# Layer 2's g@w_out of the last two tile pairs by seven block products

## The chip, the cores and the metric

The kernel runs on one core of a Trainium2 chip, in one launch. The metric is device time in microseconds; the median of several executions is compared. The trace and the profile are of one execution of the same program.

## What is computed

An attention over chunks of 32 rows, and two feed-forward layers behind it, all in fp32:

```python
q, k, v: (4, 8, 768, 64)      # chunk 32, 16 rows of left and 8 of right context, 8 memory rows
for c in range(768 // 32):
    scores = q_c @ concat(mem_k, k_ctx).T / 8
    out[:, :, c] = softmax(scores) @ concat(mem_v, v_ctx)
x = out.transpose(0, 2, 1, 3).reshape(3072, 512)
for layer in (1, 2):                              # w_in 512 x 2048, w_out 2048 x 512
    h = x @ w_in
    g = h * clip(h + 3, 0, 6) / 6                 # layer 1
    g = where(h >= 1, h, where(h <= -1, 0, (h + 1)**2 / 4))   # layer 2
    x = g @ w_out
```

## The kernel before

**Tiles.** The 3072 tokens are six tiles of 512 (T). d_ff is 16 blocks f of 128 (NF), d_model four chunks of 128 (NC). Each fp32 operand is split into two fp32r parts (a high part by a ScalarE cast, a low part by a VectorE subtraction), and a product is three matmuls: high by high, high by low, low by high. The function `split` does this for g; it writes ghi and glo, of which there are three buffers each.

**Stages.** Attention of the first tile and the packed weights come first, then layer 1 of tiles 0 and 1 in the direct way (`hidden`, `project`) with attention of the others in between. The rest is five tile pairs, numbered by layer (0 or 1) and pair: (0,1), (0,2), (1,0), (1,1), (1,2). The text says "layer 2" for l = 1.

**A pair.** For eight i (each two blocks f) `hidden_pair` makes h = x @ w_in of both tiles by seven products of half-size blocks instead of eight (Strassen's scheme in Winograd's form): operands A11, A12, S1 to S4, A22 made by `pair_x` on VectorE and ScalarE out of the two tiles of x, weights B11, B21, B22, T1 to T4 made beforehand by `combine` and `weight_pair`. Each product is six matmuls (2 chunks x 3) into a PSUM bank X, W or Z, with ScalarE copies and VectorE additions between products. `gate` applies the activation: ScalarE (relu, and in layer 2 a square) and VectorE. The pair's first tile goes through `project` as g comes out; the second tile's g is kept in SBUF (g_parts) and goes through `project` after the last i, 16 blocks f after one another, while the next pair's operands are made.

**w_out in layer 2.** `project` lets g stand and w_out move: y[128 tokens, 512] += ghi[:, 128 tokens].T @ w_out, for four token chunks, three matmuls each. y has four PSUM banks ("y"); the hidden products have four others ("h", "a"). After the last f each y is copied to SBUF and stored, 256 KB at a time.

**Weights.** They come packed in 64-bit words and are unpacked (`decoded`) on ScalarE and VectorE; layer 2's w_out is unpacked by `weight(1, f, 1, ...)` beside pair (1,0), used there, and written back to DRAM (`wos`) for later loads of 512 KB by `load_out`.

**Order.** A planner (`Plan`) writes out the order of every engine's instructions ahead: each task has a key (its due place), a cost in ns and buffers out of pools: "w" has 32 slots of 4 KB a partition, "in" and "lv" two larger ones each. A share such as ("wo", 5) limits how many slots one kind of buffer may hold. Engines then run these orders strictly, and all loads and stores go through one queue, SP's.

Of the kernel before, what the change touches and what calls it, by code (L numbers as in the profile page):

```python
# [36 lines left out]
T = 512  # L37
# [194 lines left out]
def dve(n, fast=False):  # L232
    return 70 + n / (1.92 if fast else 0.96)


def act(n, psum=False):
    return (30 if psum else 60) + n * 0.9
# [3 lines left out]
def fused_kernel(ctx: ExitStack, tc: tile.TileContext, qkv, qk, vv, wpk, const, out):  # L241
# [23 lines left out]
    wfs = dram.tile([NF // 2, 4, 128, 1024], F32, name="wfs")  # L265
    wos = dram.tile([2, NF, 128, 2, 512], F32, name="wos")

    plan = Plan({**shapes, **banks})
# [24 lines left out]
    def decoded(l, f, z, key, after, raw):  # L293
# [27 lines left out]
        return lo, hi  # L321

    def weight(l, f, z, key, after=()):
# [7 lines left out]
        lo, hi = decoded(l, f, z, key, after, raw)  # L331

        def high(e):
            cast(e, tile_of(w)[:, 0], words(raw)[2][:, 1])

        def low(e):
            t = tile_of(w)
            V.tensor_tensor(out=t[:, 1], in0=words(raw)[2][:, 1], in1=t[:, 0], op=ALU.subtract)

        add(("ACT", 560), key - 0.2, high, [hi], [(w, 0)])  # L340
        t = add(("DVE", dve(512)), key - 0.1, low, [hi, (w, 0)], [(w, 1)])
        if l == 0:
            last_w.append(t)
        if l:
            keep(l, f, z, key + 1)

    def keep(l, f, z, key, after=()):
# [70 lines left out]
    def weight_pair(i, key, after):  # L418
# [31 lines left out]
        for x, b in enumerate(bs):  # L450
            m = 256 * b.shape[1]
            add(
                ("SP", 430), key + 0.2, lambda e, x=x, b=b, m=m: nc.sync.dma_start(
                    wfs[i, x, :, :m], flat(tile_of(b)).bitcast(F32)),
                [(b, y) for y in range(1 + x // 2)], [("wfs", i, x)], kb=m / 2,
            )

# [340 lines left out]
    def project(l, n, f, key, w, ghi, glo, first, last):  # L798
# [154 lines left out]
    def gate(l, p, t, f, key, h, psum=False):  # L953
        r = Buf(["r"], [128, T], F32, "r")
        if t == 0:
            g, view = h, (lambda: tile_of(h))
        else:
            if (l, p, f // 2) not in g_parts:
                g_parts[l, p, f // 2] = Buf(["w"], [128, 2, T], F32, "g")
            g = g_parts[l, p, f // 2]  # L960
            view = lambda: tile_of(g)[:, f % 2]
# [7 lines left out]
        of = (h, 0) if t == 0 else (g, f % 2)  # L969
        add(("DVE", dve(T)), key + 0.1, lambda e: V.scalar_tensor_tensor(  # L970
            out=view(), in0=tile_of(r), scalar=1.0 if l else 6.0, in1=tile_of(h), op0=ALU.min,
            op1=ALU.max if l else ALU.mult,
        ), [(r, 0)] + [(h, 0)] * t, [of])
        raw_g[l, p, t, f] = view, of

    raw_g = {}


# [47 lines left out]
    for n, (l, p) in enumerate(pairs):  # L1026
        base = NK + 30 * n
        for i in range(NF // 2):
            k = base + step * i
            if n:  # L1030
                load_pair(l, p, i, k - 6, [done[n - 1, i]])
            elif i > 1:
                combine(i, k - 2, [done[0, i - 2 if i < KEPT else i - 3]])
            done[n, i] = hidden_pair(l, p, i, k - 1.2 * (n == 4 and i == NF // 2 - 1))
            for x in range(2):
                f = 2 * i + x
# [6 lines left out]
                project(l, 2 * p, f, key, w, *split(key - 1.5, *raw_g[l, p, 0, f]), f == 0, f == NF - 1)  # L1043
        for j in range(NF):
            f = (j + NF - 4) % NF
            key = base + 24.75 + 0.5 * j
            w = w_of[f] if j < 4 else load_out(l, f, key - 5, [done[n, j // 2]])
            project(l, 2 * p + 1, f, key, w, *split(key - 2, *raw_g[l, p, 1, f]), j == 0, j == NF - 1)
        if n + 1 < len(pairs):
            pair_x(*pairs[n + 1], base + 25, [done[n, 5]])  # L1050
        if n == 1:
            for i in range(NF // 2):
                weight_pair(i, base + 4 + 3 * i, [done[1, max(i - 1, 0)]])
                for x in range(2):
                    weight(1, 2 * i + x, 1, base + 30 + step * (i + 0.5 * x) - 3, [done[1, 6]])

# [98 lines left out]
```

## Time and profile before

| | us |
|---|---|
| median of 3 runs (lowest, highest) | 1117.31 (1115.94, 1119.04) |
| the profiled execution, and its span from first to last instruction | 1116.86, 1114.8 |
| TensorE busy, weight loads busy | 1078.8, 880.1 |
| VectorE busy, ScalarE busy | 678.4, 601.7 |

Busy time is the union of an engine's instructions. A matmul's listed duration is longer than the distance to the next one's start, so instructions of TensorE overlap and its busy time hides small gaps. The rows that matter stand below.

### The profile page before, as it was taken

What the parts mean: (1) busy time and instruction counts of PE and PEld (TensorE: products, weight loads), DVE (VectorE), ACT (ScalarE), POOL (GpSimd) and SP (SyncE); (2) the same over time, 40 slices, a digit from 0 to 9 for tenths busy, and PEclk for the clock granted to TensorE, in tenths of its full rate; (3) what the DMA queues carried; (4) which work ended last, traced back from release to release, by engine and by line L of the source; (5) the groups of instructions that cost most, each with busy time, mean ns of one, the idle gap of its engine ahead of it and who ended that gap; (6) DMA issues with size and microseconds to landing.
All of it is one profiled execution on the core that took longest, in us unless ns stands there. A gap on an engine that the chain in (4) does not pass through costs nothing.

```text
span 1114.8 us, 21047 instructions
## 1 busy us (share of the span) xinstructions
PE 1078.8 (97%) x8323; PEld 880.1 (79%) x8323; DVE 678.4 (61%) x1185; ACT 601.7 (54%) x1312; POOL 0.2 (0%) x4
## 2 busy tenths in 40 slices
PE   4699999999999999999999999999999999999998
PEld 4578888777787788888878888888888888888887
DVE  2589648866997976487797465572344562443442
ACT  3499534554665554376675477672455652555531
POOL 0000000000000000000000000000000000000000
PEclk9999999999999999999999999999999999999999
DMA  6792159887977739499999497754576264764061
GB/s 195 263 399 68 42 192 342 295 288 257 314 253 253 249 85 374 146 388 412 414 384 414 173 335 244 267 180 170 215 270 215 104 227 177 274 229 139 1 245 38
DMA packets 108808, 265.63 MB, mean 238 GB/s; under 512 B 11046, under 2 KB 44710, under 8 KB 108710
## 3 DMA queue, kind: packets, MB, share of 16 engines
q1 hardware_dynamic: 108710, 264.29, 65.9%
q8 instruction: 66, 1.08, 0.4%
q14 instruction: 32, 0.26, 0.1%
HBM read 199.23 MB, written 65.01 MB: 237 GB/s over the span
## 4 chain that ended last, share of the span: by engine, by line
PE 75%; DMA 9%; DVE 9%; ACT 3%; issue 2%; SPq 1%; DVEq 0%; ACTq 0%
PE ph L926 9%; PE ph L927 9%; PE ph L928 9%; PE po L815 8%; PE po L813 8%; PE po L814 8%; PE py L808 5%; PE py L809 5%; PE py L810 5%; PE pv L688 2%; PE ph L772 2%; PE ph L773 2%; PE ph L774 2%; DVE tr L667 2%; PE sc L619 1%
## 5 line engine op out<-in xcount | busy, mean ns | idle before, releaser
L926 PE MATMUL ph<-xop,wf 128*128 128x512 f32 x448 | 174.9, 390 | 0.8 <-ACT s L910 0.4
L927 PE MATMUL ph<-xop,wf 128*128 128x512 f32 x448 | 174.3, 389 | 0.0
L928 PE MATMUL ph<-xop,wf 128*128 128x512 f32 x448 | 174.3, 389 | 0.0
L962 ACT ACTIVATE r<-s,bias 128x512 f32<-128x512 f32 x120 | 86.7, 724 | 130.1 <-DVE s L914 129.2
L808 PE MATMUL py<-ghi,w 128*128 128x512 f32 x384 | 152.0, 396 | 0.5 <-DVE ysb L835 0.5
L809 PE MATMUL py<-glo,w 128*128 128x512 f32 x384 | 150.0, 391 | 1.1 <-DVE glo L793 1.1
L815 PE MATMUL po<-w,glo 128*128 128x512 f32 x384 | 149.6, 389 | 0.0
L810 PE MATMUL py<-ghi,w 128*128 128x512 f32 x384 | 149.6, 389 | 0.0
L813 PE MATMUL po<-w,ghi 128*128 128x512 f32 x384 | 149.5, 389 | 0.0
L814 PE MATMUL po<-w,ghi 128*128 128x512 f32 x384 | 149.4, 389 | 0.0
L914 DVE TENSOR_TENSOR s<-s,ph 128x512 f32<-128x512 f32 x120 | 82.0, 685 | 72.2 <-PE ph L928 47.2
L793 DVE TENSOR_TENSOR glo<-g,ghi 128x512 fp32r<-128x512 f32 x80 | 54.7, 690 | 97.5 <-ACT ghi L792 97.4
L792 ACT CAST ghi<-g 128x512 fp32r<-128x512 f32 x80 | 49.2, 622 | 110.6 <-PE po L814 78.6
L926 PEld LDWEIGHTS ph<-xop,wf 128*128 128x128 f32 x448 | 84.1, 188 | 19.7 <-ACT s L910 1.3
L928 PEld LDWEIGHTS ph<-xop,wf 128*128 128x128 f32 x448 | 84.1, 188 | 17.6
L927 PEld LDWEIGHTS ph<-xop,wf 128*128 128x128 f32 x448 | 84.1, 188 | 17.3
L910 ACT COPY s<-ph 128x512 f32<-128x512 f32 x120 | 69.6, 580 | 48.1 <-PE ph L928 44.2
L970 DVE SCALAR_TENSOR_TENSOR s<-r,s 128x512 f32<-128x512 f32 x80 | 55.2, 690 | 49.6 <-ACT r L966 42.4
L808 PEld LDWEIGHTS py<-ghi,w 128*128 128x128 f32 x384 | 72.0, 188 | 16.9 <-DVE ysb L835 1.0
L793 DVE TENSOR_TENSOR glo<-s,ghi 128x512 fp32r<-128x512 f32 x80 | 55.1, 690 | 49.7 <-ACT ghi L792 49.5
L809 PEld LDWEIGHTS py<-glo,w 128*128 128x128 f32 x384 | 72.1, 188 | 16.3 <-DVE glo L793 2.0
L815 PEld LDWEIGHTS po<-w,glo 128*128 128x128 f32 x384 | 72.1, 188 | 15.6 <-DVE glo L793 0.6
(94 smaller groups left out, 1723.4 us busy)
## 6 DMA issues: line engine op xcount, KB each, us to landing
w<-wos SPq DMA_DIRECT2D x124, 512.0 KB
raw<-wpk SPq DMA_DIRECT2D x64, 512.0 KB
wf<-wfs SPq DMA_DIRECT2D x48, 512.0 KB
wf<-wfs SPq DMA_DIRECT2D x48, 384.0 KB
wos<-w SPq DMA_DIRECT2D x32, 512.0 KB
wis<-w SPq DMA_DIRECT2D x16, 512.0 KB
wts<-wt SPq DMA_DIRECT2D x16, 512.0 KB
wf<-wts SPq DMA_DIRECT2D x16, 512.0 KB
```

The lines of the kernel that those rows point to most:

```text
L793: add(("DVE", dve(T)), key + 0.1, lambda e: V.tensor_tensor(out=tile_of(glo), in0=g(), in1=tile_of(ghi), op=ALU.subtract,), [of, (ghi, 0)] ...
L808: P.matmul(y, w2hi, gh, start=first, stop=False)
L809: P.matmul(y, w2hi, gl, start=False, stop=False)
L810: P.matmul(y, w2lo, gh, start=False, stop=last)
L813: P.matmul(y, gh[:, t], wt[:, 0], start=first, stop=False)
L814: P.matmul(y, gh[:, t], wt[:, 1], start=False, stop=False)
L815: P.matmul(y, gl[:, t], wt[:, 0], start=False, stop=last)
L914: add(("DVE", dve(T)), key + 0.39 * j, lambda e: V.tensor_tensor(out=tile_of(s), in0=tile_of(s), in1=tile_of(b), op=ALU.add,), [(b, 0)], [ ...
L926: P.matmul(q, whi()[:, m], xh, start=first, stop=False, skip_group_check=True)
L927: P.matmul(q, whi()[:, m], xl, start=False, stop=False, skip_group_check=True)
L928: P.matmul(q, wlo()[:, m], xh, start=False, stop=c == 1, skip_group_check=True)
L962: add(("ACT", 750 if l else act(T, psum) + 80), key, lambda e: A.activation(out=tile_of(r), in_=tile_of(h), func=AF.Relu, bias=bias[:, l:l ...
```

## The change

For the pairs (1,1) and (1,2) (`SEVEN`) the product g @ w_out is made by seven block products too. The blocks are: rows, the pair's two tiles; inner dimension, f blocks of even and odd index; columns, the two halves of 256 of w_out's permuted columns. One group d takes four blocks f (4d to 4d + 3, the two i = 2d and 2d + 1), with two products x of the scheme accumulated in one bank. w_out now stands (128 columns) and the split operand of 512 tokens moves, so results have output columns on partitions and tokens along the free dimension.

- `combine_out` makes T1 to T4 of w_out, beside pair (1,0), where w_out is unpacked, splits them and stores them (`wcs`). The unpacked w_out itself is stored with its columns permuted (`by_chunk`), so that `project` in pair (1,0) reads it in runs of 32 columns.
- `gate` keeps g of both tiles in g_parts for these pairs (at most nine buffers).
- `out_pair` runs the seven steps of a group: loads of the weights (`load_step`), S1 to S4 on VectorE (`made`), splits, 12 matmuls a step, and additions of PSUM results into SBUF sums (`c_sum`). After a pair's last group VectorE transposes 32 x 32 blocks and SP stores the result. In each group 14 results are taken out of PSUM.
- The last group of (1,2) is `out_last`: direct, both tiles one after the other, with the sums added, transposed and stored at the end, by SP and ScalarE's queues.
- Keys are moved: hidden blocks of these pairs are 3.5 apart in place of 2.75, and the pairs start earlier.

```diff
+        to = (lambda h: by_chunk(tile_of(w)[:, h])) if l else (lambda h: tile_of(w)[:, h])
...
+    def combine_out(i, raws, key):
...
+        less(0, lambda: low(0, 0), lambda: half(0, 1), lambda: half(0, 0), tops)
+        less(1, lambda: low(0, 1), lambda: half(1, 1), lambda: four(low(0, 0)), tops)
+        less(2, lambda: low(1, 0), lambda: half(1, 1), lambda: half(0, 1), tops)
+        less(3, lambda: low(1, 1), lambda: half(1, 0), lambda: four(low(0, 1)), [*tops, (raws[0], "lo")])
+        for x in range(2):
...
+            add(("ACT", act(512) + 30), key - 0.2, lambda e, of=of, to=to: A.copy(to(hi), of()), [(raws[x], "lo")], [(hi, x)])
+            add(("DVE", dve(512)), key - 0.1, lambda e, of=of, to=to: V.tensor_tensor(
+                out=to(lo), in0=of(), in1=to(hi), op=ALU.subtract,
+            ), [(raws[x], "lo"), (hi, x)], [(lo, x)])
+        for h, b in enumerate((hi, lo)):
+            add(
+                ("SP", 430), key + 0.3, lambda e, h=h, b=b: nc.sync.dma_start(
+                    wcs[i // 2, :, :, i % 2, h].rearrange("s p c -> p s c"), tile_of(b).bitcast(F32)),
+                [(b, 0), (b, 1)], [("wcs", i, h)], kb=512,
+            )
...
-                P.matmul(y, gh[:, t], wt[:, 0], start=first, stop=False)
-                P.matmul(y, gh[:, t], wt[:, 1], start=False, stop=False)
-                P.matmul(y, gl[:, t], wt[:, 0], start=False, stop=last)
+                whi, wlo = (wt[:, h].rearrange("p (k g j) -> p g k j", k=4, g=4) for h in range(2))
+                y = y.rearrange("p (g k j) -> p g k j", g=4, k=4)
+                P.matmul(y, gh[:, t], whi, start=first, stop=False)
+                P.matmul(y, gh[:, t], wlo, start=False, stop=False)
+                P.matmul(y, gl[:, t], whi, start=False, stop=last)
...
+    STEPS = (
+        ("A12", "B21", "Z"), ("A11", "B11", "X"), ("S1", "T1", "W"), ("S2", "T2", "X"),
+        ("S3", "T3", "X"), ("A22", "T4", "X"), ("S4", "B22", "W"),
+    )
+    ENDS = {"A12": [("Z", 0, 0)], "A11": [("X", 0, 0)], "S1": [("W", 1, 1)], "S2": [("X", 0, 1)], "S3": [("X", 1, 1)], "A22": [("X", 1, 0)], "S4": [("W", 0, 1)]}
...
+        for u, (x_, w_, z) in enumerate(STEPS):
+            w = load_step(p, d, w_, key + u - 5, after)
+            units = []
+            for x in range(2):
+                at = key + u + 0.5 * x
+                of, dep = made(x, x_, at - 1)
+                units.append((x, at, *split(at - 1, of, dep)))
...
+            tasks = [(x, at, gh, gl, k) for x, at, gh, gl in units for k in range(2)]
+            for x, at, gh, gl, k in tasks:
+                b = banks_of[z][k]
...
+                    P.matmul(q, wt[:, 0, m], xh, start=begin, stop=False, skip_group_check=True)
+                    P.matmul(q, wt[:, 0, m], xl, start=False, stop=False, skip_group_check=True)
+                    P.matmul(q, wt[:, 1, m], xh, start=False, stop=end, skip_group_check=True)
...
+            for z_, t, c in ENDS[x_]:
+                for k in range(2):
+                    b, o, at = banks_of[z_][k], into(k, t, c), key + u + 0.6
+                    part = c_sum[p, t, c], k
+                    if d == 0 and part not in o_buf:
+                        o_buf[part] = True
...
+                    else:
+                        add(("DVE", dve(T)), at, lambda e, b=b, o=o: V.tensor_tensor(
+                            out=o(), in0=o(), in1=tile_of(b), op=ALU.add,
+                        ), [(b, 0)], [part])
...
+        for t, order in ((1, (2, 3, 0, 1)), (0, (0, 1, 2, 3))):
+            for v in range(2):
+                o = Buf(["w"], [128, 8, 4, 32], F32, "osb", ("osb", 4))
+                for k in order:
+                    part = c_sum[p, t, k // 2], k % 2
+                    add(("DVE", 450), key + 6.8, lambda e, t=t, v=v, k=k, o=o: V.transpose(
+                        tile_of(o)[:, :, k], into(k % 2, t, k // 2)()[:, 256 * v:256 * v + 256],
+                    ), [part], [(o, k)])
...
-        base = NK + 30 * n
+        base = NK + 30 * n - 0.75 * (n == 3) - 2.75 * (n == 4)
+        seven = (l, p) in SEVEN
         for i in range(NF // 2):
-            k = base + step * i
+            k = base + (STEP7 if seven else step) * i
...
+            if seven and i % 2:
+                d = i // 2
+                out_pair(p, d, base + 2 * STEP7 * (d + 1) + 0.25, [done[n, max(i - 1, 0)]], n == 4 and d == NF // 4 - 1)
```

In `out_last` the end of one tile reads:

```diff
+            for k in range(4):
...
+                add(("DVE", dve(T)), ku, lambda e, c=c, b=bank[k]: V.tensor_tensor(
+                    out=c(), in0=c(), in1=tile_of(b), op=ALU.add,
+                ), [(bank[k], 0)], [part])
+                add(("DVE", 635), ku + 0.1, lambda e, c=c, k=k, o=o: V.transpose(tile_of(o)[:, :, k], c()), [part], [(o, k)])
+            for ks in ((0, 1, 2, 3),) if t else ((0, 1, 2), (3,)):
+                for g in range(4):
+                    add([("SP", 430), ("ACT", 430)] if t == 0 else ("SP", 430), at + 2.2, store_out(n + t, o, ks, g), [(o, k) for k in ks], kb=64 * len(ks))
```

## Rows read from the trace of the kernel before

**Rows 1.** The page: the span, and each engine's busy time, share and instructions.
```profile
span 1114.8 us, 21047 instructions
...
PE 1078.8 (97%) x8323; PEld 880.1 (79%) x8323; DVE 678.4 (61%) x1185; ACT 601.7 (54%) x1312; POOL 0.2 (0%) x4
```

**Rows 2.** Windows by tile pair: length, busy us and instructions by engine, clock, DMA.
```profile
459.00:622.00 163.00, 161.56 (x708) 132.41 (x708) 121.02 (x194) 101.88 (x166) 0.00 (x0) 1.00 0.95 371
622.00:785.00 163.00, 162.88 (x716) 133.96 (x715) 88.21 (x129) 95.11 (x153) 0.00 (x0) 1.00 0.66 232
785.00:948.00 163.00, 163.00 (x720) 134.96 (x720) 75.71 (x105) 82.47 (x129) 0.00 (x0) 1.00 0.56 207
948.00:1111.50 163.50, 162.98 (x719) 134.50 (x717) 65.53 (x97) 72.74 (x117) 0.00 (x0) 1.00 0.42 154
```

**Rows 3.** Timeline of TensorE in pair (1,0): start, duration, line, tiles.
```profile
701.11 0.39 PE L813 MATMUL po<-w,ghi 128*128 128x512 f32 x1
701.34 0.39 PE L814 MATMUL po<-w,ghi 128*128 128x512 f32 x1
701.56 0.39 PE L815 MATMUL po<-w,glo 128*128 128x512 f32 x1
701.79 0.39 PE L926 MATMUL ph<-xop,wf 128*128 128x512 f32 x1
702.02 0.39 PE L927 MATMUL ph<-xop,wf 128*128 128x512 f32 x1
```

**Rows 4.** The page: costliest groups (count, busy us, mean ns, idle before).
```profile
L813 PE MATMUL po<-w,ghi 128*128 128x512 f32 x384 | 149.5, 389 | 0.0
```

**Rows 5.** Timeline of VectorE: instructions that follow one another without a wait.
```profile
329.84 0.68 DVE L970 SCALAR_TENSOR_TENSOR g<-r,ph 128x512 f32<-128x512 f32 x1
330.44 0.68 DVE L914 TENSOR_TENSOR s<-s,ph 128x512 f32<-128x512 f32 x1
...
338.23 3.14 DVE L667 STREAM_TRANSPOSE tr<-st 32x256 f32<-32x256 f32 x7
...
878.81 1.22 DVE L864 TENSOR_TENSOR xraw<-xraw 128x1024 f32<-128x1024 f32 x1
879.95 0.68 DVE L914 TENSOR_TENSOR s<-s,ph 128x512 f32<-128x512 f32 x1
```

**Rows 6.** Windows of 40 us in which VectorE is busy most; columns as in rows 2.
```profile
290.00:330.00 40.00, 38.99 (x405) 30.83 (x405) 36.67 (x75) 23.62 (x67) 0.00 (x0) 1.00 0.87 300
...
530.00:570.00 40.00, 40.00 (x178) 33.14 (x177) 30.67 (x48) 26.67 (x43) 0.00 (x0) 1.00 1.03 414
570.00:610.00 40.00, 39.20 (x174) 32.08 (x173) 34.42 (x52) 28.16 (x46) 0.00 (x0) 1.00 1.01 394
```

**Rows 7.** Groups by line and shape: single operations that the change also uses.
```profile
L792 ACT CAST ghi<-g 128x512 fp32r<-128x512 f32 x80 | 49.2, 622 | 110.6 <-PE po L814 78.6 <-PE py L810 31.2 <-DVE glo L793 0.7
...
L428 DVE TENSOR_TENSOR raw<-raw 128x256 f32<-128x256 f32 x32 | 12.5, 422 | 0.4
...
L663 DVE STREAM_TRANSPOSE tr<-st 128x512 f32<-128x512 f32 x8 | 5.7, 707 | 0.1
...
L442 ACT CAST wp<-raw 128x512 fp32r<-128x512 f32 x8 | 5.3, 665 | 0.0
```

**Rows 8.** The window of 100 us with the most DMA traffic; columns as in rows 2.
```profile
500.00:600.00 100.00, 99.01 (x435) 81.30 (x434) 82.52 (x131) 69.71 (x112) 0.00 (x0) 1.00 1.02 405
```

**Rows 9.** Pieces of the chain that ended last: start, us, what.
```profile
273.03 2.41 DMA ymid<-ysb
...
411.54 2.68 DMA xmid<-xt
...
1111.02 0.69 DVE osb L833
```

**Rows 10.** The stores of the output: ns shortest, median, longest, first and last start.
```profile
L839 SPq DMA_DIRECT2D out<-osb x24: 332/338/622, 742.4 to 1111.7; - x24
```

More of the change, by code (lines that the diff above doesn't have):

```diff
@@ L266, in fused_kernel @@
     wos = dram.tile([2, NF, 128, 2, 512], F32, name="wos")
+    wcs = dram.tile([NF // 4, 4, 128, 2, 2, 256], F32, name="wcs")
     plan = Plan({**shapes, **banks})
@@ L331, in weight @@
         lo, hi = decoded(l, f, z, key, after, raw)
+        to = (lambda h: by_chunk(tile_of(w)[:, h])) if l else (lambda h: tile_of(w)[:, h])
+        of = (lambda: in_rows(words(raw)[2][:, 1])) if l else (lambda: words(raw)[2][:, 1])
         def high(e):
-            cast(e, tile_of(w)[:, 0], words(raw)[2][:, 1])
+            cast(e, to(0), of())
         def low(e):
-            t = tile_of(w)
-            V.tensor_tensor(out=t[:, 1], in0=words(raw)[2][:, 1], in1=t[:, 0], op=ALU.subtract)
+            V.tensor_tensor(out=to(1), in0=of(), in1=to(0), op=ALU.subtract)
         add(("ACT", 560), key - 0.2, high, [hi], [(w, 0)])
@@ L968, in gate @@
             ), [], [(r, 0)])
[L969 removed]
+        of = (g, f % 2) if own else (h, 0)
         add(("DVE", dve(T)), key + 0.1, lambda e: V.scalar_tensor_tensor(
@@ new lines, in fused_kernel, with load_step @@
+    SLOT = {"T1": 0, "T2": 1, "T3": 2, "T4": 3}
+    c_sum, o_buf = {}, {}
+    def load_step(p, d, name, key, after):
+        w = Buf(["w"], [128, 2, 2, 256], F32R, "ws", ("wo", 5))
+        if name in SLOT:
+            add(
+                ("SP", 430), key, lambda e: nc.sync.dma_start(tile_of(w).bitcast(F32), wcs[d, SLOT[name]]),
+                [("wcs", 2 * d + x, h) for x in range(2) for h in range(2)], [(w, 0), (w, 1)], kb=512, after=after,
+            )
+            return w
+        c = 256 * (name == "B22")
+        for x in range(2):
+            f = 4 * d + 2 * x + (name != "B11")
+            add(
+                ("SP", 430), key, lambda e, x=x, f=f: nc.sync.dma_start(
+                    tile_of(w)[:, x].bitcast(F32), wos[1, f, :, :, c:c + 256]),
+                [("wos", 1, f)], [(w, x)], kb=256, after=after,
+            )
+        return w
@@ new lines, in store_out, with go, out_last, chunk @@
+    def store_out(tile, o, ks, g, e="SP"):
+        def go(e):
+            eng = nc.scalar if e == "ACT" else nc.sync
+            a, b = 128 * g + 32 * ks[0], 128 * g + 32 * ks[-1] + 32
+            eng.dma_start(
+                out[tile * T:(tile + 1) * T, a:b].rearrange("(b t) c -> t b c", t=32),
+                tile_of(o)[32 * g:32 * g + 32, :, ks[0]:ks[-1] + 1].rearrange("p b k j -> p b (k j)"),
+            )
+        return go
+    def out_last(p, d, key, after):
+        n = 2 * p
+        ws = [load_out(1, 4 * d + j, key - 5 + 0.3 * j, after) for j in range(4)]
+        for t in (1, 0):
+            at = key + 2 * (1 - t)
+            o = Buf(["xhi", "xlo"], [128, T // 32, 4, 32], F32, "osb")
+            bank = [Buf(["y"] if t == 0 else ["h", "a"], [128, T], F32, "po") for _ in range(4)]
+            gs = []
+            for j in range(4):
+                gs.append(split(at + 0.5 * j - 1, *raw_g[1, p, t, 4 * d + j]))
+            jobs = [(at + 0.5 * j + 0.01 * k, j, k) for j in range(2 + 2 * t) for k in range(4)]
+            if t == 0:
+                jobs += [(at + 1 + 0.25 * k + 0.1 * (j - 2), j, k) for k in range(4) for j in (2, 3)]
+            for ku, j, k in jobs:
+                def chunk(e, j=j, k=k, w=ws[j], b=bank[k], ghi=gs[j][0], glo=gs[j][1]):
+                    q, xh, xl, wt = tile_of(b), tile_of(ghi), tile_of(glo), tile_of(w)
+                    m = slice(128 * k, 128 * k + 128)
+                    P.matmul(q, wt[:, 0, m], xh, start=j == 0, stop=False)
+                    P.matmul(q, wt[:, 0, m], xl, start=False, stop=False)
+                    P.matmul(q, wt[:, 1, m], xh, start=False, stop=j == 3)
+                add(
+                    ("PE", 680), ku, chunk, [(ws[j], 0), (ws[j], 1), *((b, 0) for b in gs[j])], [(bank[k], 0)], line="out",
+                )
+            for k in range(4):
+                c = lambda k=k, t=t: tile_of(c_sum[p, t, k // 2])[:, k % 2]
+                part = c_sum[p, t, k // 2], k % 2
+                ku = at + (1.25 + 0.25 * k if t == 0 else 2 + 0.01 * k)
+                add(("DVE", dve(T)), ku, lambda e, c=c, b=bank[k]: V.tensor_tensor(
[5 more added lines that the diff above has]
+                    add([("SP", 430), ("ACT", 430)] if t == 0 else ("SP", 430), at + 2.2, store_out(n + t, o, ks, g), [(o, k) for k in ks], kb=64 * len(ks))
@@ L1033, in fused_kernel @@
                 combine(i, k - 2, [done[0, i - 2 if i < KEPT else i - 3]])
-            done[n, i] = hidden_pair(l, p, i, k - 1.2 * (n == 4 and i == NF // 2 - 1))
-            for x in range(2):
+            done[n, i] = hidden_pair(l, p, i, k)
+            if seven and i % 2:
+                d = i // 2
+                out_pair(p, d, base + 2 * STEP7 * (d + 1) + 0.25, [done[n, max(i - 1, 0)]], n == 4 and d == NF // 4 - 1)
+            for x in range(2 * (not seven)):
                 f = 2 * i + x
@@ L1043, in fused_kernel @@
                 project(l, 2 * p, f, key, w, *split(key - 1.5, *raw_g[l, p, 0, f]), f == 0, f == NF - 1)
-        for j in range(NF):
+        for j in range(NF * (not seven)):
             f = (j + NF - 4) % NF
-            key = base + 24.75 + 0.5 * j
+            key = base + 24.75 + (0.72 if n == 2 else 0.5) * j
             w = w_of[f] if j < 4 else load_out(l, f, key - 5, [done[n, j // 2]])
@@ L1053, in fused_kernel @@
                 weight_pair(i, base + 4 + 3 * i, [done[1, max(i - 1, 0)]])
-                for x in range(2):
-                    weight(1, 2 * i + x, 1, base + 30 + step * (i + 0.5 * x) - 3, [done[1, 6]])
+                raws = [weight(1, 2 * i + x, 1, base + 30 + step * (i + 0.5 * x) - 3, [done[1, 6]]) for x in range(2)]
+                combine_out(i, raws, base + 30 + step * (i + 0.5) - 2)
     with tc.manual_schedule():
```

87 lines of the change are left out of this document (82 added, 5 removed).

## The prediction

> **What bounds the kernel now.** The page's busy shares come first: TensorE 97%, VectorE 61%, ScalarE 54% of the span [rows 1]. A mean over stages is not enough, so next come windows cut by tile pair: four stretches of 163 us, for the pairs (0,2), (1,0), (1,1), (1,2). In (1,1) TensorE starts 720 matmuls, VectorE is busy 75.7 us, ScalarE 82.5 us, the DMA engines 0.56 [rows 2]. The TensorE timeline shows what a slot is: matmuls are listed with 0.39 us each but start 0.2267 us apart, and the w_out products and the hidden products keep the same pace [rows 3]. So 163 us hold 163 / 0.2267 = 719 starts: TensorE has no gap there, and each removed matmul is worth 0.2267 us. Since a listed matmul outlasts its slot by 0.16 us, small gaps don't show in busy time; I count starts.
>
> **What is removed.** g@w_out cost 2 tiles x 16 f x 4 x 3 = 384 matmuls a pair (one of its three lines has 384 over three pairs [rows 4]). Four f blocks by seven products of 12 matmuls are 84 in place of 96. Pair (1,1) has four such groups: 336. Pair (1,2) has three, and a last group done directly: 252 + 96 = 348. Removed: 48 + 36 = 84, x 0.2267 = **19.0 us**, if everything else hides. The new ones also have 128 columns standing and 512 moving, so I give them the same pace.
>
> **What is added beside pair (1,0).** combine_out gives VectorE, for each of eight i, four 256-wide subtractions (0.42 us [rows 7]) and two 512-wide (back to back they start 0.60 apart [rows 5]): 8 x (1.68 + 1.20) = 23.0 us. VectorE goes from 88.2 to 111.2 of 163, from 54% to 68%. At 54% 716 of 719 slots were used (0.7 us empty), at 74% in (0,2) 708 (2.5 us empty) [rows 2]. Interpolated: 0.7 of the way, (2.5 - 0.7) x 0.7 = **+1.3 us**, bounds 0 and 2.5. ScalarE's 16 casts of 0.665 [rows 7] make 95 into 106 of 163, no bound. The 16 stores of 512 KB raise 232 GB/s to (37.8 + 8.4 MB) / 163 us = 283 GB/s; 405 GB/s went by while TensorE was busy 99 of 100 us [rows 2, 8]: nothing. If that cover goes, each store waits in SP's queue for its subtraction, behind it wait the next loads of hidden weights, and then TensorE; this sits in the upper bound.
>
> **Strided moving operand.** Pair (1,0)'s 384 w_out matmuls now stream w_out in 16 runs of 32 words. No row shows this form. From the contiguous row's 0.2267 [rows 3] I take nothing, and the bound above by the slowest listed time, 0.39 per matmul: 384 x 0.16 = 63 us. It is a rival, not a term. [...]
>
> **VectorE in pairs (1,1) and (1,2).** One cycle is two hidden blocks i and one group of four f: 84 + 84 matmuls, 38.1 us of TensorE. VectorE's 512-wide instructions in it: 14 for the hidden blocks as before, 8 operand sums, 14 splits (8 before), 14 additions out of PSUM: 50 x 0.60 = 30.0 us, 79%. Stretches with such a load: 77% (530 to 570 us) with TensorE busy 40.0 of 40; 86% (570 to 610) with 39.2; 92% (290 to 330) with 39.0 [rows 6]. ScalarE takes 24 more casts a pair, 82.5 + 16 = 98 of 152 us: not the bound.
> The additions bring a wait: S3 may not write bank X before VectorE has read S2's result from it, and A22 not before S3's. Behind the waiting matmul stands all of TensorE's queue. The two banks alternate: bank 0 is done 0.68 us before the step ends, an addition takes 0.69, so an idle VectorE costs about nothing and a queue of one instruction 0.6 us, unless a hidden product (1.36 us) lies between. Over the four cycles away from the change of pair (152 us) I take 1% for all this, **+1.5 us**; bounds 0 (the 77% row) and 2% = 3.0 (the 86% row).
>
> **The change from (1,1) to (1,2).** Until now 192 matmuls of the pair's second tile, 43.5 us with little VectorE work, covered the making of the next pair's operands. That cover is gone. Into one cycle fall the 11 operations of pair_x (1.14 apart [rows 5], 12.5 us) and 16 transposes (seven took 3.14 us [rows 5], so 0.45 each, 7.2 us): 30.0 + 12.5 + 7.2 = 49.7 us of VectorE against 38.1 of TensorE. The sums of (1,2) also take the four buffers that (1,1)'s sums leave only when transposed. The most VectorE reached in a stretch is 92% [rows 6]. If the excess spreads over the cycle and its two neighbours: (30.0 + 49.7 + 30.0) / 0.92 = 119.2 against 114.3, **+4.9 us**. Bounds: 0 (spread over all seven cycles, 229.7 / 0.92 = 250 against 267) and 49.7 / 0.92 - 38.1 = 15.9 (nothing spreads). I take the middle case since the split buffers and operands let the work slide by about a group. The change from (1,0) to (1,1) keeps (1,0)'s light tile as cover and costs nothing.
>
> **The tail.** Today the last copy (0.69) ends at 1111.71 and the store ends the span at 1114.8 [rows 9, 10]. After: an addition of the same length, a transpose (0.707 [rows 7]), then four stores over two queues, the second of a queue 0.34 later [rows 10]. Those stores write 4 x 512 runs of 128 bytes. Of two 256 KB stores one with 128 runs landed in 2.41 us, one with 512 in 2.68 [rows 9]: 0.7 ns a run, so 1,536 more runs are 1.1 us. Tail **+2.2 us**, bounds 0.7 (the transpose alone) and 2.8 (one queue). [...]
>
> **Sum.** -19.0 + 1.3 + 1.5 + 4.9 + 2.2 = -9.1 us against the profiled execution's 1116.86 (its span of 1114.8 and 2.1 around it), so 1107.8; that execution is 0.45 below the median, and I say **1108**. With all lower bounds -18.3 (1098.6), with all upper ones +5.2 (1122).
>
> **Rivals.** *VectorE's gaps absorb everything* (0.26): the terms of 1.3, 1.5 and 4.9 shrink to a third; about -14 to -18, 1099 to 1103. For it: (1,1) and (1,2) lose no slot today and seven cycles average 86%. Against: 49.7 us in one cycle.
> *VectorE sets the pace* (0.17), the one on the other side: an in-order VectorE that waits for ScalarE's casts and for PSUM attains less than 92%. Its seven cycles hold 229.7 us; at attained share u they last 229.7 / u. The gain is gone at 266.7 + 15.5 = 282.2, u = 81%; below that the kernel is slower, at 78% by 12 us (1129). About half of this case lies below 81%. For it: 62% to 74% was all that VectorE did in (0,2) with slots lost; against: the 86% and 92% stretches.
> *The strided operand* (0.07): every 10% on 384 matmuls costs 8.7 us; at 10% the sum is zero, at 20% 1117 + 8. For it: no row shows that it is free. Against: ScalarE's cast out of every second word takes 0.665, one out of neighbouring words 0.622 [rows 7], so a coarser pattern than this costs another engine 7%.
>
> **Chances and range.** My case (1103 to 1114) has 0.46, absorbed 0.26, VectorE's pace 0.17, strided 0.07, and 0.04 goes to loads that come late for lack of buffers: at the change of pair g may hold 9, xop 6, wo 5, wf 8, xraw 5 and osb 4 of the working pool's 32 slots, 37 in all (1110 to 1120). 0.3% is 3.4 us, about what a measurement of this kernel can tell from no change. Faster (under 1114): 0.46 + 0.26, 0.02 of VectorE's pace and 0.02 of late loads, 0.76. Same: 0.06 of VectorE's pace, 0.04 strided, 0.02 late loads, 0.12. Slower: 0.09 and 0.03, 0.12. The range 1099 to 1118 leaves out the slower half of VectorE's pace, most of the strided case and a little at the lower end, 0.18.
>
> **What would show it.** TensorE: 336 and 348 w_out matmuls in the last two pairs, 0.2267 apart. (1,0) as long as before within 2 us, with its w_out matmuls at the same pace. Few gaps in (1,1); one stretch of gaps around the change to (1,2), ended by VectorE, with VectorE over 90%. A tail of 6 us after the last matmul in place of 3.8. I am wrong if gaps spread evenly over both pairs (VectorE's pace), if (1,0) is longer (strided operand), or if gaps end on loads (buffers).

## The result and the profile after

The changed kernel takes 1108.94 us (median of 11 runs, 1102.90 to 1113.98), the kernel before 1118.28 (11 runs, 1115.94 to 1121.87). The ratio is 0.9916, 95% interval 0.9892 to 0.994: about 9.4 us faster, of 9.3 predicted from the median of the runs shown first (1117.31 to 1108). The profiled execution took 1102.90 and is the shortest of the eleven; where most of its 6 us under the median lie is seen below (e1).

The page of the kernel after, to be read against [rows 1]; the last line is one of the new product lines (count, busy us, mean ns, idle time before):

```profile
span 1101.1 us, 21263 instructions
...
PE 1061.2 (96%) x8239; PEld 864.4 (79%) x8239; DVE 817.3 (74%) x1439; ACT 634.0 (58%) x1376; POOL 0.2 (0%) x4
...
L1155 PE MATMUL po<-glo,ws 128*128 128x512 f32 x196 | 76.3, 390 | 0.0
```

TensorE's count falls from 8323 to 8239, the 84 of the prediction: three product lines of 196 and three of 32 for the direct last group make 684 = 336 + 348. VectorE gains 139 us of work, 61% to 74%.

Windows of the kernel after, columns as in [rows 2]: the first four by tile pair, then the two stretches in which VectorE is busiest, then the tail.

```profile
459.00:622.00 163.00, 161.80 (x710) 132.73 (x709) 129.37 (x216) 109.69 (x178) 0.00 (x0) 1.00 1.02 393
622.00:785.00 163.00, 161.57 (x698) 130.58 (x697) 101.05 (x157) 100.45 (x162) 0.00 (x0) 1.00 0.79 276
785.00:940.00 155.00, 155.00 (x683) 127.94 (x682) 130.05 (x198) 93.35 (x151) 0.00 (x0) 1.00 0.60 202
940.00:1101.00 161.00, 152.09 (x672) 125.68 (x670) 126.66 (x207) 80.62 (x136) 0.00 (x0) 0.98 0.48 149
890.00:930.00 40.00, 40.00 (x178) 33.04 (x177) 39.91 (x58) 28.25 (x45) 0.00 (x0) 1.00 0.68 222
930.00:970.00 40.00, 40.00 (x179) 33.12 (x178) 39.18 (x71) 24.57 (x42) 0.00 (x0) 1.00 0.52 146
...
1093.00:1099.00 6.00, 0.00 (x0) 0.00 (x0) 0.57 (x1) 0.00 (x0) 0.00 (x0) 0.63 0.98 174
```

Pair (1,0) starts 698 matmuls in its 163 us where it started 716. Pair (1,1) loses none: 155 / 0.2267 = 684, and 683 are there. Around the change from (1,1) to (1,2) VectorE is busy 39.91 and 39.18 of 40 us, and TensorE still starts 178 and 179. In the tail, from the end of the last transpose (1093.57) on, no engine computes, and in this window the DMA engines are busy 0.98 at 174 GB/s. The same view of the kernel before, at its own end:

```profile
1110.50:1113.50 3.00, 0.48 (x3) 0.06 (x1) 1.21 (x2) 0.00 (x0) 0.00 (x0) 1.00 0.94 350
```

At a share of 0.94 the engines carried 350 GB/s there, twice the 174. The TensorE timeline of pair (1,0) after, against [rows 3]:

```profile
790.98 0.40 PE L858 MATMUL po<-w,ghi 128*128 128x512 f32 x1
791.21 0.40 PE L859 MATMUL po<-w,ghi 128*128 128x512 f32 x1
791.45 0.40 PE L860 MATMUL po<-w,glo 128*128 128x512 f32 x1
791.68 0.40 PE L858 MATMUL po<-w,ghi 128*128 128x512 f32 x1
```

From the first to the last are 0.70 us: 0.2333 apart, not 0.2267. These are the w_out matmuls, which stream w_out in 16 runs. The hidden matmuls right behind them are slower too:

```profile
770.10 0.39 PE L971 MATMUL ph<-xop,wf 128*128 128x512 f32 x1
...
771.49 0.40 PE L858 MATMUL po<-w,ghi 128*128 128x512 f32 x1
```

Six hidden matmuls take 1.39 us here, 0.2317 each. Over all of (1,0), leaving out distances over 0.26 us, the first nine hidden matmuls behind a group of w_out matmuls start 0.2311 apart in the mean and the later ones 0.2266; in the kernel before both are at 0.2267.

To split the difference I cut both executions at the same events: the first w_out matmul of (1,0), the first seven-block product, the last matmul, the end of the span. The rows that give them (shortest/median/longest ns, first and last start), first of the kernel before, whose last matmul, the third of its product, starts at 1110.6:

```profile
L813 PE MATMUL po<-w,ghi x384: 389/389/504, 631.1 to 1110.1; 128*128 128x512 f32 x192
...
L815 PE MATMUL po<-w,glo x384: 388/389/504, 631.5 to 1110.6; 128*128 128x512 f32 x192
```

and of the kernel after, in which (1,0), the products and the direct last group have a line each:

```profile
L858 PE MATMUL po<-w,ghi x128: 394/396/398, 626.5 to 802.9; 128*128 128x512 f32 x128
...
L1154 PE MATMUL po<-ghi,ws x196: 388/389/393, 804.9 to 1069.5; 128*128 128x512 f32 x196
...
L1084 PE MATMUL po<-ghi,w x32: 388/389/390, 1070.6 to 1091.7; 128*128 128x512 f32 x32
```

| us | before | after | difference |
|---|---|---|---|
| start to the first w_out matmul of (1,0) | 631.1 | 626.5 | -4.6 |
| from there to the last matmul | 479.5 | 465.2 | -14.3 |
| last matmul to the end of the span | 4.2 | 9.4 | +5.2 |

The first piece holds work that the change hardly touches: combine_out begins in it, at 589.5 us, and from 600 to 626 us TensorE starts 116 matmuls in both kernels. The other two give -14.3 + 5.2 = -9.1 us: the predicted sum, but with other terms in it. The middle piece should have lost 19.0 and lost 14.3, and the tail grew by 5.2, not 2.2. One wait of TensorE in 600 to 800 us is new (us, times, longest); the same view of before lists none there:

```profile
PE ph L971 <- DVE s L959: 1.4, 1, 1.4
```

The middle piece can be split further by the distances between starts, counted over the whole trace. It has 2,111 of them before and 2,027 after: the 84 saved matmuls, 19.0 us. What the distances have beyond 0.2267 us is 1.0 us before (0.1 in slower matmuls, 0.9 in gaps) and 5.7 after: 3.6 in slower matmuls (2.6 in those of w_out, 1.0 in the hidden ones behind them) and 2.1 in gaps, nearly all of it in (1,0). So of the 4.7 us that the middle missed, the slower pace is 3.5 and more gaps are 1.1.

### The profile page after: what moved, and what is told of

The parts are those of the page before. It is cut to its first block, busy times and chain, and to the rows that moved or that the text cites. A ratio compares the mean times of both kernels' runs of the same rounds, so it can differ in the third digit from the quotient of the medians.

```text
span 1101.1 us, 21263 instructions
## 1 busy us (share of the span) xinstructions
PE 1061.2 (96%) x8239; PEld 864.4 (79%) x8239; DVE 817.3 (74%) x1439; ACT 634.0 (58%) x1376; POOL 0.2 (0%) x4
## 4 chain that ended last, share of the span: by engine, by line
PE 69%; DMA 14%; DVE 9%; ACT 3%; issue 3%; SPq 1%; DVEq 0%; ACTq 0%
PE ph L971 8%; PE ph L972 8%; PE ph L973 8%; PE py L851 5%; PE py L852 5%; PE py L853 5%; PE po L1155 4%; PE po L1154 4%; PE po L1156 4%; PE po L859 3%; PE po L858 3%; PE po L860 3%; DMA wfs<-wp 2%; PE pv L731 2%; PE ph L815 2%
## 5 line engine op out<-in xcount | busy, mean ns | idle before, releaser
L835 ACT CAST ghi<-g 128x512 fp32r<-128x512 f32 x126 | 77.0, 619 | 89.4 <-PE po L859 26.2
L836 DVE TENSOR_TENSOR glo<-g,ghi 128x512 fp32r<-128x512 f32 x126 | 85.2, 687 | 52.4 <-ACT ghi L835 51.6
L851 PEld LDWEIGHTS py<-ghi,w 128*128 128x128 f32 x384 | 72.1, 188 | 16.3 <-DVE ysb L880 0.5
L853 PEld LDWEIGHTS py<-ghi,w 128*128 128x128 f32 x384 | 72.1, 188 | 15.2
L1155 PE MATMUL po<-glo,ws 128*128 128x512 f32 x196 | 76.3, 390 | 0.0
L1154 PE MATMUL po<-ghi,ws 128*128 128x512 f32 x196 | 76.3, 389 | 0.0
L1156 PE MATMUL po<-ghi,ws 128*128 128x512 f32 x196 | 76.3, 389 | 0.0
L1016 DVE SCALAR_TENSOR_TENSOR g<-r,s 128x512 f32<-128x512 f32 x72 | 49.6, 688 | 20.1 <-ACT r L1012 17.4
L687 ACT ACTIVATE st<-sc,sm 128x64 f32<-128x64 f32 x192 | 57.3, 325 | 10.7 <-DVE sm L682 10.3
```

The lines of the kernel that those rows point to most:

```text
L836: add(("DVE", dve(T)), key + 0.1, lambda e: V.tensor_tensor(out=tile_of(glo), in0=g(), in1=tile_of(ghi), op=ALU.subtract,), [of, (ghi, 0)] ...
L1154: P.matmul(q, wt[:, 0, m], xh, start=begin, stop=False, skip_group_check=True)
L1155: P.matmul(q, wt[:, 0, m], xl, start=False, stop=False, skip_group_check=True)
L1156: P.matmul(q, wt[:, 1, m], xh, start=False, stop=end, skip_group_check=True)
```

## The experiments

They ask for three things: what took 4.7 us out of the middle piece, why the tail costs 5.2, and how near VectorE came to being the bound. In each, the theories are numbered for that run alone. "Middle" and "tail" are the pieces of the table; "(1,0)" is the time from its first w_out matmul to the first seven-block product, 804.9 - 626.5 = 178.4 in the kernel after, and "the rest" the 286.8 that follow up to the last matmul. Where a kernel has one run only, its pieces are compared and not its total.

**The changed kernel once more (e1), no edit.**

> The changed kernel once more, unedited, for a second trace. Theory 1 (the change's own effect is fixed; the rest of a run's time varies in the stages that the change doesn't touch): from pair (1,0) on, the pieces are as in the first trace within 1 us (pairs (1,1) and (1,2) without a lost slot, 9 us from the last matmul to the end), and a difference in total lies before 430 us. Theory 2 (VectorE at 98% has no reserve, so an execution loses now and then): gaps of several us in (1,1) and (1,2).

1107.05 us (1103.94 to 1113.33), ratio 0.9917 [0.9891, 0.9943]. Its profiled execution has the same (1,0), rest and tail (178.4, 286.8, 9.4) and a first w_out matmul at 631.3, not 626.5. So the 4.6 us of the first row of the table are scatter between executions of one kernel, and the gain is what the other two rows give.

**w_out in neighbouring words (e2).** The permutation moves from the matmul's moving operand to the copy out of PSUM.

> Pair (1,0)'s w_out moves as it lies in SBUF, in one run of 512, and the columns are put in order by the copies out of PSUM. Theory 1 (the pattern of the moving operand costs): w_out matmuls in (1,0) start 0.2267 apart again in place of 0.233, 384 x 0.006 = 2.4 us off (1,0), total 0.998 of the changed kernel. Theory 2 (combine_out's work and stores slow every matmul in that stage): pitch and length of (1,0) stay.

```diff
-                whi, wlo = (wt[:, h].rearrange("p (k g j) -> p g k j", k=4, g=4) for h in range(2))
-                y = y.rearrange("p (g k j) -> p g k j", g=4, k=4)
+                whi, wlo = (wt[:, h] for h in range(2))
...
+                    if l:
+                        cast(e, in_rows(tile_of(o)), by_chunk(tile_of(y)))
```

1106.67 us (1100.66 to 1112.33), ratio 0.9906 [0.988, 0.9933], no shorter than e1 by its interval. The w_out matmuls are back at 389 ns, but (1,0) took 179.0. What the faster matmuls gave went into gaps: of the distances between starts, 0.1 us is slower pace now (3.6 in the kernel after), 4.6 are gaps (2.1) and 1.6 come from matmuls about 0.43 us apart (none). TensorE's waits in 600 to 800 us:

```profile
PE ph L970 <- DVE s L958: 2.3, 1, 2.3
PE ph L970 <- ACT s L954: 1.4, 2, 1.2
```

The chain of this run around the longer one (start, us, what):

```profile
708.64 9.53 DMA xraw<-ymid
...
718.26 0.12 DVE xsum L908
...
720.01 1.22 DVE xraw L908
721.23 0.60 DVE w L347
721.83 0.61 DVE s L958
722.48 0.50 PE ph L970
...
723.23 0.43 PE ph L972
723.66 0.43 PE ph L970
```

Read from the top: a load of the next pair's x lands at 718.2; the operand sum of L908, which it releases, starts at 718.3 on VectorE, and a second one at 720.0; behind them stands the addition of a hidden block (L958), and TensorE waits for that. VectorE had stood idle 3.3 us for this load (2.7 in the kernel after, 1.2 in the kernel before). After TensorE's wait of 2.3 us the matmuls start 0.43 us apart for some 3.5 us, about 1.9 times the 0.23 that the chain has before the wait and behind them; the 40 us from 720 have a granted clock of 0.96, the 40 us before and after them 1.00. So the moving operand's pattern is one cost in (1,0), and a late load of x is another.

**The pattern alone, in the kernel before (e3).** All three pairs of layer 2, 1,152 matmuls, read w_out in 16 runs; the splits write the permuted order, and nothing else changes.

> The kernel before with one part of the change: layer 2's w_out lies permuted in SBUF and moves in 16 runs of 32 words, in all three pairs of layer 2 (1,152 matmuls), without combine_out and without the seven products. Theory 1 (the pattern costs): 0.233 in place of 0.2267, so 1,152 x 0.006 = 7 us slower. Theory 2 (it doesn't, the slower pace in (1,0) is contention): no change.

```diff
+                whi, wlo = (wt[:, h].rearrange("p (k g j) -> p g k j", k=4, g=4) for h in range(2))
+                y = y.rearrange("p (g k j) -> p g k j", g=4, k=4)
...
-            cast(e, tile_of(w)[:, 0], words(raw)[2][:, 1])
+            cast(e, to(0), of())
```

1125.17 us (1124.0 to 1129.05), ratio 1.0079 [1.0063, 1.0095]: +8.8 us. The TensorE timeline of this run:

```profile
1104.78 0.40 PE L820 MATMUL po<-w,ghi 128*128 128x512 f32 x1
1105.01 0.40 PE L821 MATMUL po<-w,ghi 128*128 128x512 f32 x1
1105.25 0.40 PE L822 MATMUL po<-w,glo 128*128 128x512 f32 x1
1105.48 0.40 PE L820 MATMUL po<-w,ghi 128*128 128x512 f32 x1
```

Again 0.2333 apart. 1,152 x 0.0066 = 7.6 us; so the pattern costs 2.9% a matmul. The hidden matmuls right behind them are slow here too (0.2308 in the mean for the first nine) and hold another 2.4 us, without combine_out and without the seven products. The two make 10.0, within the interval of the measured 8.8 (7.0 to 10.6). In the changed kernel they make 2.6 + 1.0 = 3.6 us, and with w_out in neighbouring words (e2) both are gone. Why the hidden matmuls, whose own operands lie as before, are slower was not tested.

**The last tile stored in halves (e4).** The stores of the last tile take chunks (0, 1) and (2, 3), with runs of 256 bytes, where they took (0, 1, 2) with 384 and (3) with 128.

> The last tile's stores as two halves of two column chunks (runs of 256 bytes) in place of three chunks and one (384 and 128 bytes). Same 4,096 runs. Theory 1 (the stores go at a pace per run): 2,048 runs still wait for the last transpose as now; from the last matmul to the end 9.0 us as now, within 0.5. Theory 2 (bytes set the pace): 256 KB more wait, at the 170 KB per us that were seen 1.5 us later. Theory 3 (runs under some length are slower each): about 1 us earlier.

```diff
-            for ks in ((0, 1, 2, 3),) if t else ((0, 1, 2), (3,)):
+            for ks in ((0, 1, 2, 3),) if t else ((0, 1), (2, 3)):
```

One run, 1106.59 us; the tail is 7.2 us in place of 9.4. The window of its tail:

```profile
1097.00:1103.00 6.00, 0.97 (x5) 0.47 (x3) 2.37 (x4) 0.00 (x0) 0.00 (x0) 0.96 0.98 182
```

The rate is the same as after's (182 and 174 GB/s, engines full). The gain is that the stores begin while the last matmuls still run: the first of the last tile goes out at 1096.8, 0.8 us before the last matmul's start, in the kernel after 0.5 us behind it.

**No combine_out (e5).** The seven combinations of w_out are neither made nor stored; the loads take blocks of w_out that exist. The products of (1,1) and (1,2) thus get other weights and don't compute the output.

> combine_out is left out whole (VectorE, ScalarE and its 16 stores); the loads of T1 to T4 read as many bytes of the stored w_out, so the results of pairs (1,1) and (1,2) are not the reference's. Theory 1 (what (1,0) loses is the pattern of the moving operand, 384 x 0.006 = 2.4 us, and about 1 us of waits that combine_out's stores cause by delaying the loads of the next pair's x): the pitch of 0.233 stays, the gap of 1.1 to 1.6 us near 717 us is gone, (1,0) is 1 to 1.5 us shorter than in the changed kernel. Theory 2 (VectorE's load there is what costs): 3 us or more shorter. The rest as in the changed kernel.

```diff
-        hi, lo = (Buf(["w"], [128, 4, 256], F32R, f"wc{x}", ("wc", 4)) for x in range(2))
...
+        return
...
-                ("SP", 430), key, lambda e: nc.sync.dma_start(tile_of(w).bitcast(F32), wcs[d, SLOT[name]]),
+                ("SP", 430), key, lambda e: nc.sync.dma_start(
+                    tile_of(w).rearrange("p x h c -> p (x h) c").bitcast(F32),
+                    wos[1, 4 * d + SLOT[name]].rearrange("p h (x c) -> p (h x) c", x=2)),
```

One run, 1107.64 us; (1,0) takes 177.7 us in place of 178.4. The gap stays, with 1.0 us in place of 1.4:

```profile
PE ph L943 <- DVE s L931: 1.0, 1, 1.0
```

So (1,0) is 0.7 us shorter without combine_out, but that is within what (1,0) varies by: e4, which has combine_out whole and the same (1,0), takes 177.6 us, and the others with this (1,0) between that and 181.3 (e9). The gap is 1.1 in e1, the changed kernel itself. What combine_out costs is thus not resolved, and it is small; theory 2, 3 us or more, did not come. The gap stands without its stores: they are gone here.

**More VectorE work in the last two pairs (e6).** The splits of the eight operand sums subtract twice: 58 instructions of 512 a cycle, not 50.

> The changed kernel with the low-part subtraction of S1 to S4 done twice on VectorE: 8 more 512-wide instructions in each cycle of four f blocks, 58 in place of 50, 34.8 us of 38.1 (91%), and 54.5 us in the cycle with the change of pair. The seven cycles would hold 7 x 34.8 + 19.7 = 263 of 267 us. Theory 1 (VectorE can run at 98% and more without holding TensorE, as the first trace shows at 890 to 970 us, because the written order lets work slide over several cycles): lost time in (1,1) and (1,2) 0 to 4 us. Theory 2 (the prediction's: above 92% TensorE waits): 267 us become 263 / 0.92 = 286, so some 19 us lost.

```diff
-        add(("DVE", dve(T)), key + 0.1, lambda e: V.tensor_tensor(
-            out=tile_of(glo), in0=g(), in1=tile_of(ghi), op=ALU.subtract,
-        ), [of, (ghi, 0)], [(glo, 0)])
+        for _ in range(1 + twice):
+            add(("DVE", dve(T)), key + 0.1, lambda e: V.tensor_tensor(
+                out=tile_of(glo), in0=g(), in1=tile_of(ghi), op=ALU.subtract,
+            ), [of, (ghi, 0)], [(glo, 0)])
```

One run, 1118.97 us; the rest takes 295.0 us, 8.3 more, between what the theories gave. Two windows of it:

```profile
930.00:970.00 40.00, 38.29 (x162) 29.33 (x161) 39.76 (x63) 22.84 (x38) 0.00 (x0) 1.00 0.46 145
970.00:1010.00 40.00, 37.45 (x161) 29.52 (x161) 38.16 (x70) 26.02 (x44) 0.00 (x0) 1.00 0.89 289
```

VectorE is as full as in the changed kernel, but TensorE now starts 162 and 161 matmuls instead of 178: the work of the change of pair reaches into the next cycle and finds no slack (from 970 to 1010 us VectorE is busy 38.16, in the changed kernel 32.94). The reserve ends between 50 and 58 instructions a cycle. The second subtraction also makes its own operands 0.6 us later, which this run doesn't tell apart from a fuller VectorE.

**The last tile in quarters (e7).** 16 stores of 128-byte runs for the last tile.

> The last tile's stores in four parts of one column chunk each (runs of 128 bytes, 16 stores). After halves the tail was 7.2 us in place of 9.4, with 256-byte runs moved at about the same bytes per us as runs of 384, 128 and 512. Theory 1 (bytes per us are fixed at about 180 KB for these stores whatever the run, and only the start of the stream counts): the stream starts 1.4 us before the halves' second quarter, the last 256 KB take 1.4 us after the last transpose, tail 4.6 to 5.5 us. Theory 2 (issuing 16 stores of 512 runs, 0.8 us each on two queues, is the limit): 6.5 to 7.5 us.

```diff
-            for ks in ((0, 1, 2, 3),) if t else ((0, 1, 2), (3,)):
+            for ks in ((0, 1, 2, 3),) if t else ((0,), (1,), (2,), (3,)):
```

One run, 1109.97 us, tail 9.4. Its window:

```profile
1100.00:1106.00 6.00, 0.00 (x0) 0.00 (x0) 0.59 (x1) 0.00 (x0) 0.00 (x0) 0.85 0.97 133
```

Full engines move 133 GB/s. An earlier start is paid back by the rate.

**Long runs, other partitions (e8).** Each store takes 32 whole rows of the output, its outermost dimension the four column groups.

> The last pair's two tiles are stored by 32 tokens and all 128 partitions at a time (16 stores a tile, runs of 512 bytes, all four column chunks together), in place of one 32-partition group at a time. Theory 1 (32 partitions are what holds a store to 180 KB per us): the stream goes at up to 370 KB per us, 1 MB in 2.8 us after the last transpose, tail about 6 us. Theory 2 (runs of 512 bytes and shorter are what holds it): 1 MB in 5.6 us, tail about 9 us.

```diff
-                out[tile * T:(tile + 1) * T, a:b].rearrange("(b t) c -> t b c", t=32),
-                tile_of(o)[32 * g:32 * g + 32, :, ks[0]:ks[-1] + 1].rearrange("p b k j -> p b (k j)"),
+                out[r0:r0 + 32, :].rearrange("t (g c) -> g t c", g=4),
+                tile_of(o)[:, g].rearrange("p k j -> p (k j)"),
```

One run, 1122.90 us, tail 20.7; neither theory gave that. Its window:

```profile
1102.00:1118.00 16.00, 0.00 (x0) 0.00 (x0) 0.29 (x1) 0.00 (x0) 0.00 (x0) 0.58 0.29 86
```

The engines are busy 0.29 in the mean, not full. By its share it would be 86 / 0.29 = 297 GB/s with full engines, an estimate. The first of the last two tiles in the kernel after is stored with runs of 512 bytes too, but by 32 partitions at a time, and there full engines move 196:

```profile
1086.50:1090.50 4.00, 4.00 (x19) 3.34 (x18) 2.38 (x4) 0.00 (x0) 0.00 (x0) 1.00 0.98 196
```

So the partitions may count beside the length of the runs. But 297 is scaled up from a mean share of 0.29, so whether longer runs alone would restore the rate stays open.

**Both last tiles in halves (e9), and with e2's contiguous w_out (e10).**

> The changed kernel with both tiles of the last group stored in halves of two column chunks. Theory 1 (in the tail the DMA engines are full at about 180 KB per us with such runs, and the two tiles' 2 MB are one stream, so an earlier start ends it earlier): the second tile's stores start some 2.5 us earlier than with halves of the last tile alone, tail 6.0 to 6.5 us in place of 7.2 and 9.4; total about 3 us under the changed kernel, ratio 0.989. Theory 2 (only the last tile's second half counts): 7.2 us.

> As the run with both tiles in halves, and pair (1,0)'s w_out moves in one run, columns put in order by the copies out of PSUM. Theory 1 (the 2.5 us of the pattern are given back in that stage by the wait for the next pair's x, as the run with this part alone showed): (1,0) as long as in the changed kernel within 1.5 us, same total as the run with halves alone. Theory 2 (that wait was chance): 2.5 us faster than halves alone.

```diff
-            for ks in ((0, 1, 2, 3),) if t else ((0, 1, 2), (3,)):
+            for ks in ((0, 1), (2, 3)):
```

e9: 1110.36 us, ratio 0.9917 [0.9893, 0.994]; e10: 1106.90, 0.988 [0.9858, 0.9902]. The tails are 8.7 and 8.6, not e4's 7.2; the reason is seen under e11. In e9 (1,0) took 181.3 with a gap of 2.3 us at the late x and some slow matmuls behind it, of e2's kind, in e10 177.5. The gap's size differs from kernel to kernel and between executions of one (1.4, 1.1, 2.3, 0.6 and 2.3 us in the kernel after, e1, e2, e4 and e9), and it moves (1,0) as much as the pattern does. Between e9 and e10 (1,0) differs by 3.8 us, of which 3.4 are the slower pace; gaps and matmuls of that kind together hold about as much in both (5.0 and 4.7). So e10's second theory holds: the pattern's cost comes back whole when the gaps are alike.

**e10, and the uses of x later (e11).** The planner takes pair (1,1)'s loads of x as 1024 KB each, reckons with a later landing, and so puts VectorE's sums of x later in its order, with other work ahead of them. The loads themselves go out about as before: the first 75.9 us behind the first w_out matmul, in e10 76.5.

> As the run before, and the planner takes the loads of pair (1,1)'s x for twice their size, so that VectorE's written order puts their use later and other work ahead of it. Theory 1 (an operand sum that waits for its load holds VectorE, behind it the hidden block's addition and then TensorE): the gaps between 680 and 725 us are gone, (1,0) loses nothing against the kernel before, 3 to 4 us faster than halves alone, ratio 0.986. Theory 2 (the loads themselves are late for TensorE): the gap moves, the length stays.

```diff
-                of, [(b, 0)], kb=512, after=after,
+                of, [(b, 0)], kb=1024 if (l, p) == (1, 1) else 512, after=after,
```

1103.92 us (1103.52 to 1104.37), ratio 0.9855 [0.983, 0.9879]: the fastest of all. Its rows of the three kinds of w_out matmuls (here each is a line earlier):

```profile
L857 PE MATMUL po<-w,ghi x128: 389/389/397, 631.7 to 804.2; 128*128 128x512 f32 x128
...
L1153 PE MATMUL po<-ghi,ws x196: 389/389/394, 806.3 to 1070.8; 128*128 128x512 f32 x196
...
L1083 PE MATMUL po<-ghi,w x32: 388/389/389, 1072.0 to 1093.0; 128*128 128x512 f32 x32
```

(1,0) takes 806.3 - 631.7 = 174.6 us and the middle 461.3, where 479.5 - 19.0 = 460.5 is what 84 saved matmuls leave. Against e10, the same kernel without this edit, (1,0) is 3.0 us shorter and the median 3.0 lower. VectorE no longer stands idle for the load, and TensorE's wait for VectorE is gone; one wait for ScalarE is left, as e10 and e2 have it:

```profile
PE ph L970 <- ACT s L954: 1.1, 1, 1.1
```

The tail is still 8.7. Its stores of the last two tiles by queue (ns, first and last start):

```profile
L1055 SPq DMA_DIRECT2D out<-osb x12: 316/572/1372, 1085.4 to 1098.0; - x12
...
L1055 ACTq DMA_DIRECT2D out<-osb x4: 360/442/638, 1092.2 to 1095.3; - x4
```

Twelve of the sixteen went to SP's queue, the last at 1098.0, 3.8 us after the last transpose began. What held them is in the waits of that queue (us, times, longest):

```profile
SPq L1055 <- DMA out<-osb: 5.2, 2, 4.8
```

The queue stood 4.8 us until a store issued before had landed (2.2 at most in e4, 4.8 in e9 and e10 too), and from 1093.6 to 1098.6 us the DMA engines were busy 0.84 only, at 156 GB/s. So cutting the first tile's stores as well lost what the last tile's earlier start had gained. e4's tail with this middle was not run.

**The last group by seven products too (e12).**

> The last group of pair (1,2) by seven products too, with the pair's ordinary end (16 transposes of 256 columns, 16 stores of 128 KB on SP's queue) in place of the direct one. 12 matmuls fewer, 2.7 us. Theory 1 (the direct group pays by its shorter tail): after the last matmul two additions, four transposes and 1 MB or more at 180 KB per us on one queue, tail 11 to 14 us, slower in all by 0 to 3 us. Theory 2: tail as now, 2.7 us faster.

```diff
-                out_pair(p, d, base + 2 * STEP7 * (d + 1) + 0.25, [done[n, max(i - 1, 0)]], n == 4 and d == NF // 4 - 1)
+                out_pair(p, d, base + 2 * STEP7 * (d + 1) + 0.25, [done[n, max(i - 1, 0)]], False)
```

One run, 1112.79 us. With 12 matmuls (2.7 us) fewer the rest takes 287.7 us, 1.0 more, since 3.5 us of gaps have come, and the tail 11.8, 2.4 more. The direct last group of the change pays for itself.

## Why the prediction was right, and where its terms were not

**The gain.** Right. 84 matmuls at 0.2267: e11's middle is 18.2 us under before's, of 19.0, and the rest of the changed kernel loses no slot. The new products keep 389 ns.

**combine_out beside (1,0), +1.3.** Not resolved. Without it (1,0) is 0.7 us shorter (e5, a single run), less than kernels with the same (1,0) differ by.

**The strided moving operand, 0.** Mis-sized: 3.6 us, 2.6 in the w_out matmuls and 1.0 in the hidden ones behind them, by the distances of starts after and in e3. The sign named for it, a longer (1,0), came. The rival's mechanism is real, at 2.9% a matmul and not at the 10% from which it would have decided; that it reaches into the matmuls behind was not foreseen. My lower end was taken from a row of another form. Runs of 128 bytes cost 2.9% here (0.2333 us against 0.2267).

**Late loads.** I gave the mechanism 0.04 and put it at the change of pair for lack of buffers; a small form of it sits in (1,0). Gaps there cost 2.1 us in the kernel after, 1.1 more than in the kernel before, and 1.4 of them is the wait behind the late x. It stands without combine_out's stores (e5), and with the uses of x later in VectorE's order (e11) it is gone. That the change caused the 1.1 isn't shown, since the gap differs by more than that between kernels. 3.5 + 1.1 = 4.6 of the 4.7 us by which the middle missed.

**VectorE in the last pairs, +1.5 and +4.9.** Both are 0: the rest holds 1,265 distances between starts, 286.7 us at 0.2267, and lasts 286.8. The gaps around the change to (1,2) that I had named as a sign did not come. The step that failed is "the most VectorE reached in a stretch is 92%": that was the most it had been asked for. It ran at 39.91 of 40 us with TensorE full, and the excess spread over the neighbouring cycles, as my lower bound had it. The rival *VectorE's gaps absorb everything* was right on these two pairs. That VectorE could set the pace was no idle rival either: 8 instructions more a cycle cost 8.3 us (e6).

**The tail, +2.2.** Mis-sized, and outside its own bounds (0.7 to 2.8): 5.2. The transpose is as priced: the last matmul starts at 1091.71 and the last transpose ends at 1093.57, 0.75 us more than from before's last matmul to its last copy. The stores are not: 7.5 us from there to the end in place of 3.1, 4.4 more, where I had 1.5. I priced landings by their count of runs, from two stores during which the engines were busy 0.73 and 0.82, at 256 GB/s. In the tail 1 MB goes out in one stream, and the engines are full (0.98) at 174 GB/s. 1 MB at that rate is 6.0 us. With full engines, runs of 128 bytes move 133 GB/s (e7), of 384 with some of 128 behind them 174 (after), of 256 bytes 182 (e4), and of 512 bytes 196 (after, the tile before).

**The total.** -19.0 + 3.5 + 1.1 + 5.2 = -9.2, measured -9.3 by the medians. Predicted -9.1, and that the sum fits is luck: 6.4 us of VectorE's terms that didn't come stand against 3.5 of the pattern and 3.0 of the tail that I had not priced.

## What to carry to other kernels

Cut both traces at the same events before you believe a total that fits: here a right sum hid several wrong terms, and mending two of them (the moving operand's pattern, the late x) took another 3.9 us out of the middle piece, 3.5 of them the pattern's. A busy share that an engine had in the past is no ceiling for it (VectorE's 92% before was 99.8% after); add work in an experiment to find where it ends. Price the last stores of a kernel by the rate at which full DMA engines move runs of that length (here 133 GB/s for 128 bytes, 196 for 512), and a strided operand by its own pitch (here 0.2333 us), since each is seen only where nothing hides it.

## What was not expected of the hardware

- A matmul whose moving operand is read in 16 runs of 32 words starts every 0.2333 us, in neighbouring words every 0.2267, although its count of columns is the same (after and before; 0.2333 in e3 too). The first nine matmuls behind such a group, with operands in neighbouring words, start 0.2311 us apart in the mean, later ones 0.2266 (after).
- Stores to the output with runs of 128 to 512 bytes, 32 partitions at a time, keep the DMA engines 0.97 to 0.98 busy in the mean at 133 to 196 GB/s (e7, after, e4); before's stores, with runs of 2 KB, moved 350 GB/s at 0.94. A store with four as its outermost dimension ran at a busy share of 0.29 and 86 GB/s (e8).
- VectorE was busy 39.91 of 40 us (99.8%; after, 890 to 930 us), in order and fed by two other engines, while TensorE lost no slot (178 starts).
- After a wait of 2.3 us TensorE's matmuls started 0.43 us apart for about 3.5 us, and the 40 us around them have a granted clock of 0.96 (e2).
